# Two tokens a partition: pairing the chunks of two sequences in a recurrence-and-FFN kernel

## Chip, cores, metric

One core of one Trainium2 chip. The metric is the device time of one execution in microseconds (us), as the median of several; shares, chains and waits come from one profiled execution of each kernel.

## The reference

A gated linear recurrence (4 sequences, 8 heads, 768 tokens, head size 48), then a feed-forward layer with a squared ReLU on all 3072 tokens.

```python
f = 1.0 / (1.0 + np.exp(-f_logit))
for t in range(S):
    state = f[:, :, t, :, None] * state + np.einsum('bhd,bhe->bhde', k[:, :, t], v[:, :, t])
    y[:, :, t] = np.einsum('bhd,bhde->bhe', q[:, :, t], state)
x = y.transpose(0, 2, 1, 3).reshape(B * S, H * D)      # 3072 x 384
h = np.maximum(x @ w_in, 0.0)                          # 384 x 2048
return (h * h @ w_out).astype(np.float32)              # 2048 x 384
```

The inputs lie as (sequence, head, token, 48), so one head's one token is a run of 192 bytes.

## The kernel before

The recurrence runs in 24 chunks of 128 tokens of one sequence, one token a partition. A planner lists all steps with guessed durations and fixes the order of each engine's instructions at build time; `plan.add(name, engine, us, function, after=..., take=buffers, give=buffers)` is one step. "SP" steps are DMAs issued by SyncE. PE is TensorE, DVE VectorE, ACT ScalarE, POOL GpSimd.

```python
C = 128; NCH = 24; IOB = 7             # chunks; input buffers of each kind
LOADS = [0, "i0", 1, "i1", 2, "i2", 3, "i3", 4, "o0", "o1", 5, "o2", "o3"] + list(range(6, NCH))
XBAR = 14; XBAR2 = 18                  # from these chunks on, DMA transposes instead of TensorE's
UNITS = [(0, 2), (2, 1), (3, 1), (4, 1), (5, 1)] + [(c, 3) for c in range(6, NCH, 3)]

def load(i):                           # one DMA of 128 partitions for each of f, k, q, v
    b, c = divmod(i, NC)
    for n in ("f", "k", "q", "v"):
        def fn(n=n):
            t = io.tile([C, H, D], F32, tag="io_" + n, name="io_" + n)
            nc.sync.dma_start(t, srcs[n][b].rearrange("h s d -> s h d")[c * C:(c + 1) * C])
        plan.add(f"{n}{i}", "SP", 0.45, fn, take=["io_" + n], rank=0, data=(1.07, 1024))
# ... cut: a1 (ACT: exp, ln of f), p1 (PE: prefix sums, "pc"), a2p/a2n (ACT: exp)
def vc():                              # values to bf16
    nc.gpsimd.tensor_copy(vz[i % 4], st["v", i])
# ... v1k, v1q (DVE): k and q times the exponentials, into "az"
def t2():                              # transpose of az by DMA; p2 + v2 do it on PE
    nc.sync.dma_start_transpose(st["ts", i], az[i % 4].rearrange("p h d -> p (h d)"))
# ... p3 (PE "at"), v3 (DVE mask, "am"), p4 (PE "yp"), a3 ("ys"), p6/v6 or t6 ("xT")
def p5():                              # what the chunk adds to the state, "ds"
    for pr in range(NP):
        nc.tensor.matmul(ds[:, pr, :], a[:, H + 2*pr:H + 2*pr + 2, :].rearrange("p h d -> p (h d)"),
                         vt[:, 2*pr:2*pr + 2, :].rearrange("p h d -> p (h d)"), skip_group_check=True)
# ... mm1 ("hp", ReLU "hr", square "hT"), mm2 ("op", copy "ob", store)
```

## Time and profile before

| | before |
|---|---|
| median of 3 runs | 192.04 us (192.0 to 192.1) |
| span of the profiled run | 189.8 us, clock 1.0 |
| real TensorE work, by the chain's pitches (worked out in the prediction) | 160 us |
| DMA engines | full to 152 us |

The rows, windows and chain lines that carry this stand in the prediction. Two more lines of the page, the granted clock in 40 slices and the chain of work by engine, will be needed:

```profile
PEclk9999999999999999999999999999999999999999
...
PE 75%; ACT 11%; DMA 4%; SPq 3%; DVE 3%; issue 2%
```

Three quarters of the chain that ended last is TensorE's own work. DMA is full but holds the end up by only 4%.

### The profile page before, as it was taken

The page shows a single profiled execution, that of the slowest core. Times are in us where ns is not written, and L with a number is a line of the kernel's source. Part 1 is how long each engine was busy: PE and PEld are TensorE (multiplying, and loading weights), DVE is VectorE, ACT ScalarE, POOL GpSimd, SP SyncE. Part 2 cuts the span into 40 slices and gives each one's busy share as a digit, 9 for nine tenths or more (in the row PEclk, how much of TensorE's full clock was granted, in tenths as well). Part 3 has the DMA queues.
Part 4 walks back from the last instruction along what each step waited for, and adds up shares of the span by engine and source line. Part 5 has one row for each costly group of instructions (what it writes and reads, how often), then busy time and mean ns, then how long its engine had stood idle before and what let it go on. Part 6 is the DMA issues. An engine that isn't in the chain of part 4 may idle for free.

```text
span 189.8 us, 4807 instructions
## 1 busy us (share of the span) xinstructions
PE 177.5 (93%) x1845; PEld 120.8 (64%) x1845; DVE 127.6 (67%) x259; ACT 132.8 (70%) x281; POOL 54.8 (29%) x105
## 2 busy tenths in 40 slices
PE   6978689989899999999999999999999999999992
PEld 5867478767676666665656666666565666666551
DVE  5484688668397886999988777777667764343300
ACT  4426479786676469999998986978875787565521
POOL 5451343241224561305324311531324401100000
PEclk9999999999999999999999999999999999999999
DMA  6999899999979999999799999979999762211112
GB/s 122 188 191 206 174 187 153 196 164 191 205 137 221 232 227 201 207 197 159 140 155 194 207 137 241 218 109 215 194 216 177 176 60 64 62 45 41 41 41 83
DMA packets 118646, 30.26 MB, mean 159 GB/s; under 512 B 113408, under 2 KB 117760, under 8 KB 118624
## 3 DMA queue, kind: packets, MB, share of 16 engines
q1 hardware_dynamic: 113760, 23.27, 71.2%
q0 software_dynamic: 4864, 6.69, 16.4%
q8 instruction: 14, 0.23, 0.5%
q14 instruction: 8, 0.07, 0.1%
HBM read 25.17 MB, written 4.72 MB: 157 GB/s over the span
## 4 chain that ended last, share of the span: by engine, by line
PE 75%; ACT 11%; DMA 4%; SPq 3%; DVE 3%; issue 2%
PE op L489 31%; PE hp L444 30%; ACT hr L451 4%; DMA io_f<-in_f_logit_dram 4%; SPq L215 3%; PE at L342 3%; PE yp L365 3%; PE tr L318 2%; ACT hT L458 2%; PE pc L286 2%; PE xp L379 1%; PE ds L405 1%; ACT pz L276 1%; ACT e L275 1%; DVE hr L453 1%
## 5 line engine op out<-in xcount | busy, mean ns | idle before, releaser
L444 PE MATMUL hp<-xT,w_in 128*128 128x384 bf16 (+2 forms) x528 | 78.0, 282 | 2.5 <-DVE hr L453 1.9
L489 PE MATMUL op<-w_out,hT 128*128 128x384 bf16 x384 | 76.2, 326 | 0.3 <-ACT ob L499 0.3
L451 ACT ACTIVATE hr<-hp 128x384 bf16<-128x384 f32 (+1 forms) x100 | 50.5, 509 | 20.0 <-PE hp L444 18.0
L444 PEld LDWEIGHTS <-w_in 128*128 128x128 bf16 x528 | 42.3, 98 | 20.7 <-issue 4.0
L489 PEld LDWEIGHTS <-hT 128*128 128x128 bf16 x384 | 35.1, 98 | 21.8 <-issue 0.4
L460 DVE TENSOR_TENSOR hT<-hr 128x384 bf16<-128x384 bf16 (+1 forms) x75 | 29.7, 400 | 27.7 <-ACT hr L451 26.8
L349 DVE TENSOR_TENSOR am<-at,ut 128x512 bf16<-128x512 f32 x48 | 31.6, 685 | 3.7 <-PE at L342 3.4
L422 POOL TENSOR_TENSOR sz<-tm,en 48x192 bf16<-48x192 f32 x40 | 22.0, 549 | 29.9 <-DVE tm L413 7.2
L458 ACT ACTIVATE hT<-hr 128x384 bf16<-128x384 bf16 (+1 forms) x45 | 24.8, 554 | 1.6 <-DVE hr L453 0.3
L504 POOL DMA_DIRECT2D out_dram<-ob x18 | 10.4, 577 | 47.3 <-ACT ob L499 31.2
L280 POOL CAST vz<-io_v 128x384 bf16<-128x384 f32 x24 | 13.6, 567 | 31.2 <-DMA io_v<-in_v_dram 30.7
L306 DVE TENSOR_TENSOR az<-io_k,ep 128x384 bf16<-128x384 f32 x24 | 14.0, 584 | 8.3 <-ACT ep L296 5.1
L275 ACT ACTIVATE e<-io_f 128x384 f32<-128x384 f32 x24 | 12.5, 520 | 7.7 <-DMA io_f<-in_f_logit_dram 7.7
L499 ACT COPY ob<-op 128x384 f32<-128x384 f32 x18 | 8.6, 478 | 12.8 <-PE op L489 12.7
L296 ACT ACTIVATE ep<-pc 128x384 f32<-128x384 f32 x24 | 11.7, 486 | 5.8 <-PE pc L289 5.4
L310 DVE TENSOR_TENSOR az<-io_q,en 128x384 bf16<-128x384 f32 x24 | 14.7, 614 | 0.0
L276 ACT ACTIVATE pz<-e 128x384 bf16<-128x384 f32 x24 | 12.5, 523 | 0.8
L453 DVE TENSOR_SCALAR hr<-hp 128x384 bf16<-128x384 f32 (+1 forms) x20 | 11.6, 584 | 2.0 <-PE hp L444 1.8
L522 PE MATMUL idle<-zero 128*128 128x128 bf16 x119 | 11.9, 256 | 1.0 <-DVE zero L245 1.0
L302 ACT ACTIVATE en<-pc 128x388 f32<-128x388 f32 (+1 forms) x24 | 11.8, 491 | 0.0
L326 DVE COPY ts<-tr 128x1024 bf16<-128x1024 bf16 x14 | 9.6, 687 | 3.1 <-PE tr L318 2.7
L365 PE MATMUL yp<-vz,am 128*128 128x48 bf16 x192 | 9.5, 184 | 1.3 <-DVE am L349 0.8
(40 smaller groups left out, 149.4 us busy)
## 6 DMA issues: line engine op xcount, KB each, us to landing
io_f<-in_f_logit_dram SPq DMA_DIRECT2D x24, 192.0 KB, 4.5
io_k<-in_k_dram SPq DMA_DIRECT2D x24, 192.0 KB, 4.6
io_q<-in_q_dram SPq DMA_DIRECT2D x24, 192.0 KB, 4.5
io_v<-in_v_dram SPq DMA_DIRECT2D x24, 192.0 KB, 4.5
out_dram<-ob POOLq DMA_DIRECT2D x18, 192.0 KB, 3.5
w_in<-in_moe_w_in_dram POOLq DMA_DIRECT2D x4, 384.0 KB, 7.4
w_out<-in_moe_w_out_dram POOLq DMA_DIRECT2D x4, 384.0 KB, 6.9
out_dram<-ob SPq DMA_DIRECT2D x6, 192.0 KB, 1.9
```

The source lines that it names most:

```text
L275: nc.scalar.activation(e, st["f", i].rearrange("p h d -> p (h d)"), AFT.Exp, scale=-1.0)
L276: nc.scalar.activation(pz[i % 2][:, :, :D], e.rearrange("p (h d) -> p h d", d=D), AFT.Ln, bias=1.0)
L306: nc.vector.tensor_mul(az[i % 4][:, H:, :D], st["k", i], st["ep", i])
L310: nc.vector.tensor_mul(az[i % 4][:, :H, :D], st["q", i], st["en", i][:, :HD].rearrange("p (h d) -> p h d", d=D))
L349: nc.vector.tensor_mul(t, st["at", i][x], ut4)
L365: nc.tensor.matmul(o_, w, r, start=(n == 0), stop=(n == len(ops) - 1), skip_group_check=True)
L422: nc.gpsimd.tensor_mul(nx[r, :, D * x:D * (x + 1)], st["tm", i][r, :, D * x:D * (x + 1)], st["en", i][r, HD:HD + NP].unsqueeze(2).to_broad ...
L444: nc.tensor.matmul(hp[:, x, :], w_in[:, ks, (f + x) * C:(f + x + 1) * C], xT[:, ks, lo:lo + W], start=(ks == 0), stop=(ks == KS - 1), skip ...
L451: nc.scalar.activation(hr[:, :m, :], st["hp", c0, f][:, :m, :], AFT.Relu)
L458: nc.scalar.activation(st["hT", g][:, f:f + m, lo:lo + W], hr[:, :m, :], AFT.Square)
L460: nc.vector.tensor_mul(st["hT", g][:, f:f + m, lo:lo + W], hr[:, :m, :], hr[:, :m, :])
L489: nc.tensor.matmul(st["o", i], hT[:, fs, tt * C:(tt + 1) * C], w_out[:, fs, :], start=(fs == 0), stop=(fs == FS - 1))
```

## The change

Intent: the loads' 192-byte rows are the costliest traffic, so two successive tokens go in one partition and make rows of 384 bytes. 128 tokens then fill 64 partitions, and the chunks of two sequences are stacked into a pair: 12 pairs for 24 chunks. Prefix sums, exponentials, products and transposes go by halves `r` (first or second token of a partition). The values must lie one token a partition to be multiplied, so ACT issues four SBUF-to-SBUF copies a pair. The FFN goes by units of two chunks.

```diff
-    IOB = 7
-    XBAR = 14
-    XBAR2 = 18
-    UNITS = [(0, 2), (2, 1), (3, 1), (4, 1), (5, 1)] + [(c, 3) for c in range(6, NCH, 3)]
-    GC = 3
+    IOB = 4
+    XBAR = 5
+    XBAR2 = 6
+    UNITS = [(c, 2) for c in range(0, NCH, 2)]
+    GC = 2
-                nc.sync.dma_start(t, srcs[n][b].rearrange("h s d -> s h d")[c * C:(c + 1) * C])
+                t = io.tile([C, H, 2, D], F32, tag="io_" + x, name="io_" + x)
+                for j in range(2):
+                    nc.sync.dma_start(t[P2 * j:P2 * (j + 1)].rearrange("p h r d -> p h (r d)"),
+                                      srcs[x][2 * m + j][:, c * C:(c + 1) * C, :].rearrange("h (p r) d -> p h (r d)", r=2))
-            nc.gpsimd.tensor_copy(vz[i % 4], st["v", i])
+            nc.gpsimd.tensor_copy(st["vb", n].rearrange("p r h d -> p h r d"), st["v", n])
+        def vs():
+            t = st["vz", n] = work.tile([C, 2, H, D], BF16, tag="vz", bufs=3, name="vz")
+            for j in range(2):
+                for r in range(2):
+                    nc.scalar.dma_start(t[P2 * r:P2 * (r + 1), j].rearrange("p h d -> p (h d)"),
+                                        st["vb", n][P2 * j:P2 * (j + 1), r].rearrange("p h d -> p (h d)"))
+        plan.add(f"vs.{n}", "ACT", 0.4, vs, after=[f"vc.{n}"], take=["vz"], data=(0.66, 0))
+        plan.add(f"sub.{n}", "DVE", 0.47, sub, after=[f"p1.{n}"], take=["le"], give=[f"pz:a1.{n}"])
-            nc.sync.dma_start_transpose(st["ts", i], az[i % 4].rearrange("p h d -> p (h d)"))
+                for j in range(2):
+                    nc.sync.dma_start_transpose(st["ts", n][:, j, :, r, :], a[P2 * j:P2 * (j + 1), r].rearrange("p h d -> p (h d)"))
+            for pr in range(NP):                 # ds: 16 matmuls of 64 rows a pair
+                for r in range(2):
+                    for j in range(2):
+                        z = slice(P2 * j, P2 * (j + 1))
+                        nc.tensor.matmul(ds[j][:, pr, :], a[z, r, ...], vb[z, r, ...], start=(r == 0), stop=(r == 1))
 # cut: the same by halves in a1, p1, a2, v1, p2, v2; mask and prefix matrix re-ordered; stores in two halves
```

## The prediction

> **What bounds the kernel now.** I read, in order, the engine rows and slices of the page, the windows by stage, the same windows for the feed-forward matmuls alone, the chain of work, and the trace's packet records.
>
> ```profile
> PE 177.5 (93%) x1845; PEld 120.8 (64%) x1845; DVE 127.6 (67%) x259; ACT 132.8 (70%) x281; POOL 54.8 (29%) x105
> PE   6978689989899999999999999999999999999992
> DMA  6999899999979999999799999979999762211112
> DMA packets 118646, 30.26 MB, mean 159 GB/s; under 512 B 113408, under 2 KB 117760, under 8 KB 118624
> q1 hardware_dynamic: 113760, 23.27, 71.2%
> ```
>
> Two things are full at once. The DMA engines are full for the first 32 slices (152 us), with packets nearly all under 512 B. TensorE looks full from about slice 11. That "busy" has to be checked, because the group view gives 326 ns for a 384-column matmul while the chain passes 48 of them in 7.81 us, 163 ns each. So I count TensorE work from the chain's pitches:
>
> ```profile
> 178.60 7.81 PE op L489 x48
> 27.54 1.50 PE hp L444 x24
> 29.04 0.45 PE tr L318 x8
> 29.48 0.17 PE ds L405 x4
> 37.97 0.33 PE at L342 x8
> 16.04 0.32 PE pc L286
> 57.65 0.20 PE yp L365 x8
> 34.08 0.35 PE xp L379 x3
> 7.57 7.32 DMA io_f<-in_f_logit_dram
> ```
>
> Feed-forward: 384 op at 0.163 us is 62.5 us; hp has the same columns, 62.8. Attention, by pitches (pc 0.16 + 0.08 for its small ones, tr 0.45, at 0.33, ds 0.17, yp 0.20 + 0.17, xp 0.19 where dense), times the chunks that run each on TensorE (24, 20, 14, 24, 20, 24, 20, 18), is 34.7. Together 160 us of a 189.8 us span: 30 us are lost. Where, the windows tell (all engines; then matmuls of hp, then of op, alone):
>
> ```profile
> 17.00:50.00 33.00, 27.95 (x394) 22.89 (x394) 22.02 (x43) 24.07 (x45) 9.82 (x16) 1.00 1.07 179
> 50.00:92.00 42.00, 41.79 (x490) 28.89 (x487) 36.16 (x72) 33.09 (x76) 15.41 (x28) 1.00 1.02 201
> 92.00:151.00 59.00, 58.84 (x551) 36.36 (x550) 45.60 (x93) 48.06 (x108) 19.77 (x36) 1.00 1.04 184
> 17.00:50.00 33.00, 16.05 (x198) 2.07 (x3) 10.09 (x17) 1.00 1.07 179
> 17.00:50.00 33.00, 4.07 (x19) 0.00 (x0) 0.48 (x1) 1.00 1.07 179
> ```
>
> Priced by the pitches, TensorE does 25.7 us of real work in the first 50 us (the rest is filler on the tile "idle", or waiting), 134 us in the 136 us to 186, and then 3.7 us of last copy and store. So the loss is 24 us in the first 50, 2 later, 4 at the end. The first 50 us are bound by DMA: chunks, counted by 192-byte packets, are in at 5.9, 10.3, 20.6, 26.5, 35.9, 44.4 and 49.4 us; the eight weight pieces at 13.0, 16.0, 19.3, 28.9 (w_in) and 32.4, 35.8, 42.5, 45.9 (w_out). After 50 us TensorE is the bound, with DMA full beside it.
>
> **What the Trainium skill says.** "DMA: Bandwidth & Descriptors", Specifications, puts the minimum transfer for line rate at 512 B. The trace agrees that small ones are dear: a 192-byte packet takes 17.4 ns on average, 11 GB/s, a 1536-byte store packet 64 ns, 24 GB/s. The same page, Rules for kernel authors, says two transfers to disjoint partition halves gain nothing over one; the change splits each load so, and no run yet shows what that costs. The same page, "Issuing engines are not separate DMA queues", says DMAs of ACT run on the same 16 engines and spare only issue time: so the new SBUF copies are extra load on a full resource. "TensorEngine Tiling (Array Packing)" offers two row tiles for contract sizes up to 64; the trace agrees: the 64-row "at" matmuls go at 41 ns for 128 columns in pairs, where a 128-row transpose takes 56.
>
> **The change, part by part.**
> Loads: 98,304 packets of 192 B become 49,152 of 384 B. At 17.4 ns the old ones take 107 us of all 16 engines. For 384 B I interpolate between 192 B and 1536 B: 17.4 + 192 x (64-17.4)/1344 = 24 ns, so 74 us. A chunk falls from 4.45 to about 3.1 us: minus 33 us of DMA.
> DMA added: 3,072 packets of 768 B for re-laying the values, some 37 ns by the same line, 7 us; transposes move from 10 chunks to 14 (ts) and from 6 to 12 (xT), 12,544 to 18,944 packets at 30 ns, plus 12 us. Net minus 14 of some 167 us.
> TensorE: ds becomes 16 half-row matmuls a pair at about 42 ns, 0.67 us for 0.34, ten times: plus 3.4. Transposes leave it: 4 x 0.45 + 6 x 0.17: minus 2.8. Feed-forward in units of 256 columns is the same columns. Net plus 0.6: 160.4 us.
> DVE and ACT: a subtraction a pair, 12 x 0.55, plus 6.6 us; four fewer PSUM copies at 0.69 and six at 0.36, and fewer, fuller evictions (96 tiles of 512 columns against 120 smaller ones), minus some 12. ACT issues four DMAs a pair; a 128-packet store issue on SP took 0.33 us, so some 1.2 us a pair, 14 us in all, that no busy row counts.
>
> The path that decides is the start. By hand, with the order of instructions of the changed program: pair 0 lands at about 9 us instead of 5.9 for a chunk; its f at 4.4. The exponentials (0.84 + 2 x 0.52), the prefix matmul, four products of 0.56, two transposes through one bank with a 0.69 copy each, four mask products of 0.68 and a state copy of 0.55 x 2 are more serial work on DVE before the first pair can be multiplied: 19 us against 17.1 for the first hp. In ACT's order the re-laying of pair 1, which waits for its v, stands before a copy of pair 0's xT; with the weights sharing the engines (in the trace they took some 60% while both flowed) that v lands near 20, so the first hp comes at some 24 us. Then weights: all six remaining pieces are issued after pair 1's v, so the last w_in is in at about 29, the last w_out at 44. Loads: pair 2 at 35, pair 3 at 47: eight chunks where it was six. In TensorE's order the eight op of the second half of chunk 0 stand behind that last w_out. So at 44 us TensorE has done the first two pairs' hp (10.4), one chunk's op (2.6) and three pairs' attention (9.3): 22.3 us, as much as before by then (22). But from there four chunks wait with op and pair 2 with hp, and TensorE can be dense six us sooner than before.
> Span: 44 + (160.4 - 22.3) + some 3 of small stalls + 3.7 = 188.8; the timed run is 2.2 longer than the span: 191.0.
>
> **Rivals.**
> 1. DMA is the real bound and the saved 14 to 33 us show: then pairs land early, TensorE is dense from 35 us, and the time is 184 to 187. For: DMA full for 152 us. Against: TensorE was dense from 50 us anyway; only the start can pay, and there weights are half the traffic.
> 2. A new wait on ACT or SP. Issue time of the re-laying (14 us) and its waiting for v in ACT's fixed order hold back evictions of hp, which has two banks of 0.65 us; a DMA transpose took 1.2 us or more of SP to issue whatever its size, and there are now six a pair, 7 us of a 13.3 us pair, beside eight load issues. One us lost a pair makes 200 to 204. For: ACT was 94 to 96% busy from 70 to 100 us. Against: the xT still has another group's op work to hide behind.
> 3. Transposes from 64 partitions write shorter runs; if a packet took twice as long, DMA in the second half would need 17 us a pair against TensorE's 13.3 and the end would slip by 10 us or more. Nothing in the profile before shows it.
>
> **Range and chances.** The main sum gives 191.0. The start is uncertain by 4 us either way (when weights and loads share), the stalls by plus 4. So 187 to 196. Faster by 2% needs under 188.2: the start must go as in rival 1, 0.25. Slower by 2% needs over 195.9: rivals 2 and 3, 0.18. Within 2%: 0.57.
>
> **What would show it.** Right: 384-byte packets near 24 ns; first hp after 19 us; TensorE dense from some 44 us with 138 us of work left; weights done near 44. Wrong on the fast side: first hp by 17 us, or dense before 38. Wrong on the slow side: hp waiting for ACT evictions while ACT waits on DMA issues or on vb, TensorE gaps over 5 us in all after 50 us, or transposes that land later than the 3.9 us of before. DMA load per pair in the second half should be near 13 us.

## The result, and the profile after

| | before | after |
|---|---|---|
| median (range), 4 runs each on the same chip | 192.02 us (191.35 to 192.1) | **230.8 us** (229.82 to 231.23) |
| ratio, 95% interval | | 1.2021 (1.1973 to 1.207), slower |
| span of the profiled run, mean clock | 189.8 us, 1.0 | 228.8 us, 0.939 |

A ratio here is the mean time of one kernel's runs over that of the other's of the same rounds, so it is not quite the ratio of the medians quoted. Executions over 1.5% slower than the fastest of the same kernel are left out of the means. Results were right.

From the page of the changed kernel: TensorE, granted clock and DMA in 40 slices of 5.7 us, the packets, the main queue, the chain by engine and by line.

```profile
PE   7747377996998892995979589799749999999991
...
PEclk9995559999999999799999979999988999999999
DMA  6999899969729698796996699999999873121112
...
DMA packets 81175, 34.28 MB, mean 150 GB/s; under 512 B 72576, under 2 KB 80576, under 8 KB 81152
...
q1 hardware_dynamic: 71872, 24.92, 60.0%
...
DMA 32%; PE 28%; SPq 10%; ACT 9%; ACTq 5%; issue 5%; DVE 4%; POOL 4%; POOLq 0%; DVEq 0%
DMA io_v<-in_v_dram 16%; DMA vz<-vb 12%; PE op L575 12%; PE hp L530 11%; ACTq L310 5%; SPq L226 5%; SPq L390 4%; POOL vb L303 4%; ACT hr L537 2%; DMA ts<-az 2%; DMA io_q<-in_q_dram 2%; DVE az L355 2%; ACT e L296 1%; PE at L453 1%; ACT ep L344 1%
```

The packets of the main queue did fall, from 113760 to 71872. But DMA, which was full, has holes from slice 9 on, and TensorE has holes to slice 30. The chain has passed from TensorE (75%) to DMA (32%), and to SP and ACT while they issue; by line, loads of v (16%) and the new copies (12%, and 5% for their issue, L310) lead. Half-clock slices (5 tenths) stand where TensorE had been idle. The windows by stage, with the columns as in the prediction (engines' busy time, clock, DMA share, GB/s):

```profile
17.00:50.00 33.00, 25.12 (x297) 19.73 (x298) 20.27 (x38) 17.70 (x35) 7.81 (x10) 0.75 1.09 195
50.00:92.00 42.00, 33.76 (x379) 23.96 (x374) 27.25 (x55) 25.11 (x50) 13.03 (x19) 0.99 0.79 166
92.00:151.00 59.00, 49.63 (x540) 35.44 (x539) 36.23 (x69) 35.29 (x71) 16.11 (x23) 0.95 0.92 166
```

In the 42 us after 50, TensorE is busy 33.8 us (before: 41.8) and the DMA share is 0.79 (before: 1.02). Both resources that were full are now idle for part of the time. DMA did not get less to do: added up from the packet records, its packets took 185.6 us of all 16 engines, where they had taken 167.6 (the loads alone 98.0, where 74 were predicted and 107 had been); but its share fell all the same. For TensorE this is neither more work nor, outside the half-clock stretches, slower work, but waiting. Priced by pitches as in the prediction, with `ds` at the 0.33 us that its 16 matmuls took, the longer span falls so:

| TensorE lost (time less real work) | predicted | measured |
|---|---|---|
| to the point where it should be dense (44 us predicted; 50 us for measuring) | 21.7 | 31.4 |
| from there to the end (measured: to 190 us) | 3 | 35.1 |
| the end | 3.7 | 5.1 |
| work itself | 160.4 | 157.1 |
| sum = span | 188.8 | 228.8 (rounded) |

What do the loads wait for? The waits of SP's queue (who waited, line; for what; us in total, times, longest). L226 issues the loads:

```profile
SPq L226 <- DMA vz<-vb: 26.2, 10, 9.0
...
SPq L226 <- DMA io_v<-in_v_dram: 11.6, 13, 2.3
```

A load of new inputs needs nothing from a re-laying copy, and yet SP waits 26.2 us for such copies to land. In the kernel before, where L215 issues the loads, the longest entry of its load line is

```profile
SPq L215 <- POOL sz L422: 2.8, 3, 1.9
```

On the other engines, first of the kernel before, then of the changed one:

```profile
POOL vz L280 <- DMA io_v<-in_v_dram: 30.7, 14, 6.6
```

```profile
POOL vb L303 <- DMA io_v<-in_v_dram: 49.7, 8, 10.7
...
ACT e L296 <- DMA vz<-vb: 11.3, 3, 5.7
```

ACT, too, is seen to stand until copies land ahead of `e`, which reads nothing of them; the issues of the next copies, which wait for their turns, lie in between. The chain that ended last, in order of time (start, duration, what), shows the circle:

```profile
73.55 4.96 DMA vz<-vb
78.58 3.38 DMA io_v<-in_v_dram
...
84.31 0.84 POOL vb L303
85.17 0.48 ACTq L310
85.68 0.61 ACTq L310
86.33 0.68 ACTq L310
87.05 0.66 ACTq L310
```

A copy lands; then a load of v is issued and lands; POOL casts it; then ACT issues four copies; and so on.

The reason stands in the program's own listing, which the build of the kernel puts out. Every DMA issued by SP or ACT signals on one of eight semaphores, DMAHW0 to DMAHW7, which it takes in turn in the order of the program; a DMA waits until the previous user of its semaphore has landed. All 196 DMAs of SP and ACT in the changed kernel, stores and transposes too, follow this order in the listing. Below are successive issues of each engine in the changed kernel, with their waits:

```
SP   L226 DMACopy io_f<-in_f_logit_dram 64x8x96 [waits DMAHW0_49]
SP   L226 DMACopy io_f<-in_f_logit_dram 64x8x96 [waits DMAHW1_49]
SP   L226 DMACopy io_k<-in_k_dram       64x8x96 [waits DMAHW6_49]
SP   L226 DMACopy io_k<-in_k_dram       64x8x96 [waits DMAHW7_49]

ACT  L310 DMACopy vz<-vb 64x384 [waits DMAHW2_49,Pool_49]
ACT  L310 DMACopy vz<-vb 64x384 [waits DMAHW3_49]
ACT  L310 DMACopy vz<-vb 64x384 [waits DMAHW4_49]
ACT  L310 DMACopy vz<-vb 64x384 [waits DMAHW5_49]
```

SP's numbers jump from 1 to 6: turns 2 to 5 belong to ACT's copies. The next load that takes number 2 waits for a copy to land, and ACT issues that copy only when it reaches it in its fixed order, after POOL's cast. In the kernel before, SP has the eight to itself while it loads: eight loads in flight, two chunks. In the changed one eight half loads are one pair, the same bytes; but four turns in twelve are ACT's.

### The profile page after: what moved, and what is told of

It reads as the page before. It is cut to its first block, busy times and chain, and to the rows that moved or that the text cites. A ratio compares the mean times of both kernels' runs of the same rounds, so it can differ in the third digit from the quotient of the medians.

```text
span 228.8 us, 4956 instructions
## 1 busy us (share of the span) xinstructions
PE 187.2 (82%) x1913; PEld 136.9 (60%) x1913; DVE 126.6 (55%) x244; ACT 123.8 (54%) x237; POOL 59.3 (26%) x108
## 4 chain that ended last, share of the span: by engine, by line
DMA 32%; PE 28%; SPq 10%; ACT 9%; ACTq 5%; issue 5%; DVE 4%; POOL 4%; POOLq 0%; DVEq 0%
DMA io_v<-in_v_dram 16%; DMA vz<-vb 12%; PE op L575 12%; PE hp L530 11%; ACTq L310 5%; SPq L226 5%; SPq L390 4%; POOL vb L303 4%; ACT hr L537 2%; DMA ts<-az 2%; DMA io_q<-in_q_dram 2%; DVE az L355 2%; ACT e L296 1%; PE at L453 1%; ACT ep L344 1%
## 5 line engine op out<-in xcount | busy, mean ns | idle before, releaser
L530 PE MATMUL hp<-xT,w_in 128*128 128x256 bf16 x576 | 78.5, 276 | 3.5 <-ACT hr L537 3.3
L537 ACT ACTIVATE hr<-hp 128x512 bf16<-128x512 f32 x86 | 50.7, 594 | 33.9 <-PE hp L530 24.2
L530 PEld LDWEIGHTS <-w_in 128*128 128x128 bf16 x576 | 55.5, 99 | 19.3 <-issue 5.3
L546 DVE TENSOR_TENSOR hT<-hr 128x512 bf16<-128x512 bf16 x73 | 32.9, 456 | 40.8 <-ACT hr L537 40.4
L593 POOL DMA_DIRECT2D out_dram<-ob x36 | 19.3, 541 | 60.6 <-ACT ob L585 53.8
L460 DVE TENSOR_TENSOR am<-at,mask 128x512 bf16<-128x512 f32 x48 | 31.3, 682 | 4.1 <-PE at L453 4.0
L296 ACT ACTIVATE e<-io_f 128x768 f32<-128x768 f32 x12 | 10.1, 841 | 28.6 <-POOL sz L436 13.9
L303 POOL CAST vb<-io_v 128x768 bf16<-128x768 f32 x12 | 10.4, 867 | 54.6 <-DMA io_v<-in_v_dram 49.7
L436 POOL TENSOR_TENSOR sz<-tm,en 48x384 bf16<-48x384 f32 x20 | 17.0, 849 | 24.1 <-DVE tm L423 10.2
L544 ACT ACTIVATE hT<-hr 128x512 bf16<-128x512 bf16 x23 | 14.4, 633 | 0.6
```

The lines of the kernel that those rows point to most:

```text
L296: nc.scalar.activation(e.rearrange("p h r d -> p (h r d)"), st["f", n].rearrange("p h r d -> p (h r d)"), AFT.Exp, scale=-1.0)
L303: nc.gpsimd.tensor_copy(st["vb", n].rearrange("p r h d -> p h r d"), st["v", n])
L436: nc.gpsimd.tensor_mul(nx[r, :, :, D * x:D * (x + 1)], tm[r, :, :, D * x:D * (x + 1)], g.unsqueeze(3).to_broadcast([D, 2, NP, D]))
L460: nc.vector.tensor_mul(t, st["at", i][x], mask.rearrange("p y s t -> p y (s t)"))
L530: nc.tensor.matmul(hp[:, x, :], w_in[:, ks, (f + x) * C:(f + x + 1) * C], xT[:, ks, lo:lo + W], start=(ks == 0), stop=(ks == KS - 1), skip ...
L537: nc.scalar.activation(hr[:, :m, :], st["hp", c0, f][:, :m, :], AFT.Relu)
```

## The experiments

The theories: the re-laying hurts through the turns of the semaphores; or through ACT's time for issuing, or ACT's waiting for v; or the transfers of 64 partitions cost the loads; or the DMA transposes occupy SP. The bracket after a time is the median of the kernel before on the same chip. The first edits show what was changed; buffer releases that follow from it are cut. The median 195.14 in brackets is of four runs, two of them slow; ratios use fast runs alone.

**No re-laying (e2_no_relay).** Attention reads the values as they lie, so the result is wrong (relative error 1.0); everything else stays.

```diff
-        plan.add(f"vs.{n}", "ACT", 0.4, vs, after=[f"vc.{n}"], take=["vz"], data=(0.66, 0))
+        plan.add(f"vs.{n}", "POOL", 0.01, lambda: st.__setitem__(("vz", n), st["vb", n]), after=[f"vc.{n}"])
```

> The changed kernel without the re-lay copies at all: the values are used as they stand (wrong result on purpose, same shapes and work otherwise). Theory A and C: 190-203 us, a few us below the run with copies from POOL, by the 7-10 us of DMA time and the copy's latency. Theory B: 215 or more.

Measured: 206.73 us (205.48 to 209.79) [192.89], ratio 1.0702 (1.0635 to 1.0769). That lies between the ranges of the theories (190 to 203, and 215 or more). So the copies account for 24 of the 38.8 us, and 14 are left. SP's queue no longer waits for any DMA at its load line. The work done by 50 us is some 25 us again, nearly that of the kernel before; the first hp comes at 26.8 us, where it was 33.3 in the changed kernel.

**The copies on GpSimd's queue (e1_relay_pool).** Right result. In the listing these copies take turns on other semaphores, DMASW0 to DMASW7, and SP's loads go through DMAHW0 to 7 without a gap.

```diff
-                    nc.scalar.dma_start(t[P2 * r:P2 * (r + 1), j].rearrange("p h d -> p (h d)"),
+                    nc.gpsimd.dma_start(t[P2 * r:P2 * (r + 1), j].rearrange("p h d -> p (h d)"),
```

> The changed kernel with one thing moved: the SBUF copies that re-lay the values are issued by POOL (software queue, its own completion semaphores) instead of ACT. In the changed kernel SP's loads stood waiting for these copies (26.2 us in ten waits) because all DMAs of SP and ACT take turns on eight completion semaphores, and a load waits until the last DMA on its semaphore has landed. Theory A (loads chained to re-lay copies through shared semaphores): SP's waits for vz vanish, v loads are issued a pair or more ahead, the time falls from 231 to 195-208 us. Theory B (the 384-byte packets at 32 ns do not free DMA, so DMA bandwidth is the bound): at most 5 us off, 225 or more. Theory C (ACT stands waiting for v in its fixed order): falls as in A, as ACT no longer waits for vb; e2 and a later run must tell C from A.

Measured: 218.97 us (217.21 to 220.23) [192.89], ratio 1.1345 (1.1253 to 1.1438): half of the 24 us is gone; neither theory A (195 to 208 us) nor B (225 or more) foresaw that. The other half shows as waiting: TensorE for the copies, and SP at a transpose (L390) that stands in its order ahead of the loads. Part of this waiting is new: the copies now take turns with POOL's weights and stores, their issues waited 6.6 us for w_out pieces to land, and one copy took 17.4 us to land (median 4.1). From the waits of the engines, then of SP's queue:

```profile
PE yp L476 <- DMA vz<-vb: 15.2, 3, 10.5
```

```profile
SPq L390 <- DVE az L355: 22.8, 4, 16.2
```

**ACT waits but does not issue (e8_relay_pool_act_waits).** e1, and a one-column copy on ACT that reads the cast values where the issue stood, so that ACT waits for v as in the changed kernel.

```diff
+            nc.scalar.copy(dt, st["vb", n][:, 0, 0, :1])
+        plan.add(f"dm.{n}", "ACT", 0.4, dummy, after=[f"vc.{n}"])
```

> The run with the re-lay issued by POOL (219.0 us), plus one tiny ACT copy a pair that reads vb, so that ACT again stands waiting for v in its fixed order as in the changed kernel, without issuing DMAs and without the shared semaphores. Changed kernel 230.8. If ACT's waiting for v is what POOL's issue took away (theory C): 226-232. If it was ACT's issue time (31 us) and the semaphores shared with SP (theory A): 217-222.

Measured: 217.06 us (215.11 to 218.29) [193.29], ratio 1.1252 (1.1165 to 1.1339). The interval overlaps that of e1: ACT's waiting for v is not what costs, at least where the shared turns are gone.

**ACT busy nearly as long as the issues took (e13_relay_pool_act_busy).** e1, and four ACT copies of 128x384 a pair in that place.

```diff
+            for y in range(4):
+                nc.scalar.copy(dt, st["vb", n][:, y % 2].rearrange("p h d -> p (h d)"))
+        plan.add(f"dm.{n}", "ACT", 0.4, dummy, after=[f"vc.{n}"])
```

> The run with the re-lay on POOL (219.0 us) plus four ACT copies a pair of some 0.5-0.6 us each, at the place where the changed kernel has its four issues: ACT loses the time of the issues (31 us in all), no DMA and no semaphore of SP is touched. If the issue time is what makes the changed kernel 12 us slower than that run: 227-233 us. If it is the shared semaphores (SP's loads waiting for the re-lay): 217-223.

Measured: 221.23 us (220.77 to 223.07) [195.14], ratio 1.1453 (1.1309 to 1.1597), some 2 us above e1, and the intervals overlap. The 48 copies took 24.6 us of ACT. The issues did take long in the changed kernel. In the view of one line, min/median/max in ns, first and last start:

```profile
L310 ACTq DMA_DIRECT2D vz<-vb x48: 468/608/2032, 12.2 to 185.0; - x48
```

Together they held ACT for 31.3 us; but 24.6 us of extra work in ACT cost about 2 us in the end, if anything. Both e8 and e13 start from e1, which waits for its copies anyway; without such waits ACT's time might count for more, and no run shows that.

**The copies issued by ACT, but read by nobody (e14_unread_relay).** e2, and ACT still issues the four copies a pair into a tile that nothing reads. Its output is wrong, which doesn't matter for the time.

```diff
+        plan.add(f"vx.{n}", "ACT", 0.4, vs, after=[f"vc.{n}"], data=(0.66, 0))
+        plan.add(f"vs.{n}", "POOL", 0.01, lambda: st.__setitem__(("vz", n), st["vb", n]), after=[f"vc.{n}"])
```

> The run without re-lay (206.7 us; wrong result on purpose), but ACT issues the same four copies a pair into a tile that nobody reads. No matmul waits for them; only ACT's issue time, the DMA load and the eight shared semaphores are back. If these are what the re-lay costs: 218-228 us, with SP waiting for these copies. If the cost is that the product waits for the data: 206-211.

Measured: 231.96 us (230.01 to 232.85) [195.14], ratio 1.1956 (1.1747 to 1.2165). That is above the 218 to 228 expected: the whole 24 us are back, although no instruction uses what the copies bring. So attention's wait for the values is not needed for the loss; the copies' place among the other DMAs is enough. SP's queue again waits for them:

```profile
SPq L226 <- DMA vz<-vb: 25.0, 11, 7.3
```

**The same, from a constant (e15_unread_constant).** e14, but the copies read a constant tile. They still stand after the cast in the plan, but no longer wait for it on the chip. This was to break the circle load, cast, copy, load.

```diff
+    vk = const.tile([C, 2, H, D], BF16)
-                                        st["vb", n][P2 * j:P2 * (j + 1), r].rearrange("p h d -> p (h d)"))
+                                        vk[P2 * j:P2 * (j + 1), r].rearrange("p h d -> p (h d)"))
```

> As the run with the unread copies (232.0 us), at the same places in ACT's order, but the copies read a constant tile instead of the values just cast, so they need not wait for v. Same number of DMAs, bytes, ACT issues and turns on the eight semaphores; only the link from a pair's v to the loads that follow is cut. If the loop (load of v, cast, copy, next load on that semaphore) makes the loss: 207-216 us. If it is the number of DMAs, their issue time on ACT or fewer loads in flight: 225-233.

Measured: 229.33 us (227.6 to 230.97) [193.59], ratio 1.1855 (1.1771 to 1.1939). I had expected 207 to 216: missed. The circle through v is not needed.

```profile
SPq L226 <- DMA vz<-vk: 27.4, 10, 5.1
```

A copy that depends on no data still holds the loads up for 27.4 us. ACT's issue time and the bare number of DMAs, which the expectation names beside the turns, are in e13 too (221.2 us). What is left is that SP's turn comes after ACT's, and ACT arrives there when its own order of work lets it.

**The kernel before with such copies (e4_before_with_relay).** The same number of copies, 48 of 64 partitions, in the old layout: two a chunk, issued by ACT. Right result.

```diff
-            nc.gpsimd.tensor_copy(vz[i % 4], st["v", i])
+            nc.gpsimd.tensor_copy(st["vb", i], st["v", i])
+        def vs():
+            for r in range(2):
+                a = slice(64 * r, 64 * (r + 1))
+                nc.scalar.dma_start(vz[i % 4][a].rearrange("p h d -> p (h d)"), st["vb", i][a].rearrange("p h d -> p (h d)"))
+        plan.add(f"vs.{i}", "ACT", 0.2, vs, after=[f"vc.{i}"], take=["vz"], give=[f"vb:vc.{i}"], data=(0.33, 0))
```

> The kernel before plus a re-lay that changes nothing in the layout: the cast values go through an SBUF to SBUF copy of two 64-partition DMAs a chunk, issued by ACT, as in the changed kernel. Right result. Theory A and C: the old kernel now shows SP waiting for the copies and slows by 5 to 20% (202-230 us). Theory B: the copies add some 7-10 us of DMA time to an engine set that is full until 150 us, hidden behind TensorE: 192-197 us.

Measured: 215.94 us (214.92 to 218.55) [192.89], ratio 1.1183 (1.1106 to 1.126). The copies cost 23 us without any pairs or halves. Its profile fell in a slow run (218.55), so I take only dependencies from it. Here the same turns act in the other direction. In the chain in order of time, ACT's issue of a copy (L287) is released by the landing of a load of q, which it does not read:

```profile
72.55 5.80 DMA io_q<-in_q_dram
78.43 0.47 ACTq L287
78.93 2.17 ACTq L287
```

ACT, which evicts for TensorE, stands behind SP's loads; SP's queue in turn waits at the transposes for what ACT and DVE make (34.2 us for az). It does not wait for the copies at its load line, which I had expected. Which engine is seen to stand differs from kernel to kernel.

**The kernel before with half loads (e5_before_half_loads).** 192-byte rows stay; each load is issued as two DMAs of 64 partitions. Right result.

```diff
-                nc.sync.dma_start(t, srcs[n][b].rearrange("h s d -> s h d")[c * C:(c + 1) * C])
+                for j in range(2):
+                    nc.sync.dma_start(t[64 * j:64 * (j + 1)], srcs[n][b].rearrange("h s d -> s h d")[c * C + 64 * j:c * C + 64 * (j + 1)])
```

> The kernel before with each load issued as two 64-partition halves (192-byte rows as before): eight semaphores now hold one chunk in flight instead of two. Theory A in its stronger form (fewer bytes in flight hurts by itself): 3 to 8% slower, 198-207 us. If only the link to the re-lay matters: 192-196 us. Theory B says 192.

Measured: 215.07 us (214.08 to 216.38) [192.89], ratio 1.116 (1.1092 to 1.1228). That is more than the 198 to 207 us expected. Packets did not become slower (17.1 ns on average, before 17.4). What rose is the number of issues. Of the kernel before, then of e5, one load line (min/median/max ns):

```profile
L215 SPq DMA_DIRECT2D io_f<-in_f_logit_dram x24: 449/862/3354, 0.7 to 142.6; - x24
```

```profile
L216 SPq DMA_DIRECT2D io_f<-in_f_logit_dram x48: 595/633/2417, 0.7 to 168.9; - x48
```

The smallest issue took 0.45 us for 128 partitions and 0.60 for 64. By the medians an issue of 64 partitions was the shorter one (0.63 against 0.86); only together are the two halves dearer. In e5 SP spends 142 us on 192 load issues and 24 on transposes (before: 108 on 96, and 22.5), which fills 92% of its time to the last load (before: 85%), and from 50 to 110 us chunks land about every 6 us (before, from 50 to 90: every 4.7). POOL's waiting for v rises from 30.7 us to

```profile
POOL vz L281 <- DMA io_v<-in_v_dram: 79.5, 21, 7.9
```

So halving the loads is dear by itself. It adds to SP's issue time and also halves how many bytes eight semaphores keep in flight; this run does not separate the two.

**The kernel before with wide rows alone (e6_before_wide_rows).** One whole DMA of 128 partitions brings 256 tokens of one sequence in rows of 384 bytes; the kernel takes each half as if it were a chunk, so the result is wrong. It shows what wide rows can give at best.

```diff
-                nc.sync.dma_start(t, srcs[n][b].rearrange("h s d -> s h d")[c * C:(c + 1) * C])
+                nc.sync.dma_start(t.rearrange("p h r d -> p h (r d)"),
+                                  srcs[n][b][:, c * C:(c + 2) * C, :].rearrange("h (p r) d -> p h (r d)", r=2))
```

> The kernel before with only the rows widened: one DMA of 128 partitions brings two chunks of a tensor in rows of 384 bytes (tokens land in another order, so the result is wrong on purpose; the work is the same; the prefix matmul may run two chunks ahead instead of three, for the planner). It tells whether 384-byte packets are dear by themselves or because a 64-partition half writes to half the partitions. In the changed kernel a 384-byte packet took 32-35 ns where 24 were predicted, so the loads gained nothing. Theory P (the half loads are the cause): packets near 20-24 ns here, DMA under 80% busy in the middle, time 182-192. Theory Q (384-byte rows cost twice 192-byte rows whatever the shape): packets 32-35 ns, time 190-198.

Measured: 189.7 us (188.22 to 190.77) [193.29], ratio 0.9836 (0.9759 to 0.9914). Its TensorE and DMA rows:

```profile
PE   7784998999999999999999999999999999999992
...
DMA  5999999999999999995998604407253321111112
```

DMA has room from slice 22, where the kernel before was full to slice 32 (its packets took 133 us of all engines, before 167.6), and yet the time falls only by 1.6%: TensorE was dense anyway after the start. A 384-byte packet of a whole load took 26.3 ns on average here, 27.9 in e9 and 28.6 in e10 below; of a half load 31.9 in the changed kernel, 31.5 and 31.6 in e14 and e15, and 34.8 to 35.9 in e1, e2, e7, e8 and e13. The medians do not part so cleanly (22 to 26 for whole loads; 22, 26 or 35 for halves). The stores that SP issues do: a 1536-byte packet took 64 to 66 ns in whole stores (the kernel before, e4, e5, e6) and 98 to 100 in the half stores of all other runs.

**Pairs without copies and with whole loads (e9_no_relay_whole_loads).** e2, and each load is one DMA of 256 tokens of one sequence; wrong. One DMA for a pair of two sequences does not build: the access pattern has too many dimensions.

```diff
-                for j in range(2):
-                    nc.sync.dma_start(t[P2 * j:P2 * (j + 1)].rearrange("p h r d -> p h (r d)"), ...)
+                nc.sync.dma_start(t.rearrange("p h r d -> p h (r d)"),
+                                  srcs[x][(n % 12) // 3][:, (n % 3) * 256:(n % 3 + 1) * 256, :].rearrange("h (p r) d -> p h (r d)", r=2))
```

> The run without re-lay (206.7 us), with each load as one 128-partition DMA instead of two halves (rows of one sequence, wrong result on purpose). SP issues 48 loads instead of 96 and eight semaphores hold two pairs in flight instead of one. Theory I (SP's issue time and the semaphores of the halves are what is left): 188-197 us, loads issued well ahead in the second half. Rival (what is left is order and latency of the pairs themselves: PSUM banks, transposes): 202-208 us.

Measured: 194.09, 197.14, 197.73 and 200.6 us [193.29]. The last three are slow against the first, so there is no ratio; its profile, too, is of a slow run. Of e2's 206.7 us some 6 to 13 go with the halves, and with the bytes in flight, which double.

**Pairs of one sequence (e10_same_seq).** The correct form of that: a pair is two successive chunks of one sequence, one whole load for each input, the copies on GpSimd's queue as in e1, the state passed on within the pair.

```diff
+                nc.sync.dma_start(t.rearrange("p h r d -> p h (r d)"),
+                                  srcs[x][n // 3][:, (n % 3) * 256:(n % 3 + 1) * 256, :].rearrange("h (p r) d -> p h (r d)", r=2))
-            row = ((2 * (n // NC) + j) * NC + n % NC) * C
+            row = i * C
 # cut: state and its two steps by chunk, not by pair
```

> A repair with the right result: the pair is two chunks that follow each other in one sequence, so a tensor of a pair is one 128-partition load in rows of 384 bytes (48 loads instead of 96 halves); the re-lay is issued by POOL; the state passes from the first half to the second within a pair. Against the run with the re-lay on POOL (219.0 us) it takes away the halves only. If the halves cost DMA time (35 against 22 ns a packet) and SP time: 203-212 us. If the re-lay's latency and the transposes on SP are all that is left: 215-220.

Measured: 209.39 us (208.6 to 209.88) [195.14], ratio 1.0809 (1.0669 to 1.095). 9.6 us below e1, on another chip; the ratios, 1.1345 and 1.0809, say the same. So the halves cost that much in a right kernel too; the state's passing and the bytes in flight change with them and were not parted from them. This is the fastest right form of the pairs that I found. The kernel before beats it.

**Transposes by DMA two pairs later (e11_same_seq_xbar7).** e10 was seen to stand at a transpose for az for up to 20.0 us.

```diff
-    XBAR = 5
-    XBAR2 = 6
+    XBAR = 7
+    XBAR2 = 9
```

> The repair with DMA transposes from pair 7 (ts) and pair 9 (xT) on, as in the kernel before (chunks 14 and 18), which takes 8 + 6 issues of 1.2-1.4 us off SP and their load off the DMA engines, and gives TensorE 4 x 0.45 + 6 x 0.19 = 2.9 us. I expect 198-208 us: 3 us or more under the repair alone, still above the kernel before, since the re-lay stays. Rival: TensorE's added work shows fully and it is 1-3 us slower than the repair.

Measured: 210.98 us (210.39 to 211.5) [195.14], ratio 1.0904 (1.08 to 1.1008). No gain, and by the runs of this chip a loss of 1.6 us, as the rival had it; my expectation missed. That wait is where SP stands, not why it stands.

**No DMA transposes (e7_no_relay_pe_transposes).** e2 with all transposes on TensorE; wrong like e2.

```diff
-    XBAR = 5
-    XBAR2 = 6
+    XBAR = 99
+    XBAR2 = 99
```

> The run without re-lay (206.7 us), with all transposes on TensorE (XBAR and XBAR2 out of reach), so SP issues no transposes (28 + 12 of them, 55 us of its time in the run without re-lay) and never stands waiting for az ahead of a load. TensorE gets 14 x 0.45 + 12 x 0.19 = 8.6 us more work. If SP's queue paces the second half: 198-206 us, loads ahead by 5 pairs. If it does not: 212-218 us.

Measured: 203.69 us (203.15 to 204.6) [193.29], ratio 1.0558 (1.05 to 1.0617); e2 had 1.0702. Faster by 3 us, on another chip, with ratios that do not overlap, although TensorE has 8.6 us more work. A DMA transpose holds SP for at least some 1.2 us whatever its size: 28 `ts` took 38.4 us of SP and 12 `xT` 16.6 us in the changed kernel, where the kernel before spent 22.5 on both.

## Why the prediction was wrong

Predicted 191.0 us, measured 230.8, outside the range of 187 to 196, with the likeliest class missed.

**The step that failed** is how the added DMAs were priced. The prediction took them as load ("3,072 packets ... 7 us") and as ACT's issue time ("14 us in all"), and allowed "some 3 of small stalls" after the start. The runs put in its place a coupling of the issuing engines: the copies take turns with the loads on eight semaphores. With the copies gone, 24 of the 38.8 us go (e2); with copies that nobody reads, all are back (e14), even from a constant (e15); ACT's time alone brings about 2 and its waiting alone none (e13, e8). Moved to a queue outside the eight, half of the 24 remains, in part as new waiting behind the weights (e1). What no run did is give the copies semaphores of their own on ACT's queue; so that the turns are the cause is shown by SP's 26.2 us, by the listing and by exclusion of the rivals, not by a run that removed nothing else.

**The second mis-sized term** is the half load. The prediction priced its packets by interpolation at 24 ns. That is near for whole transfers (means of 26 to 29 ns) and wrong for the halves that the change uses (31.9 in the changed kernel, 35 without ACT's copies). So the loads gave DMA 9 us back (107 to 98) and not 33, and where the prediction has "net minus 14", all packets together took 18 us more (167.6 to 185.6). Halves also leave SP with 96 load issues, as many as before, where whole loads would have had 48. Against whole loads that is 9.6 us (e1 against e10, with the reserve made there). It had quoted the skill's rule on halves and written that no run showed the cost yet, and then used the whole-transfer figure.

Point by point:

- *Bound before.* Right. e6 frees DMA some ten slices earlier and gains 1.6%: only the start can pay, as said. The expected gain of 1.0 us was of the right kind; there was little to be had.
- *TensorE's work.* 160.4 predicted (its own terms, 160.0 and 0.6, add up to 160.6), 157.1 measured by the same pitches: `ds` took 0.33 us for its 16 matmuls, not 0.67.
- *The start.* First hp at 24 predicted, 33.3 measured. The pairs were to land at 9, 20, 35 and 47 us; they landed at 10.0, 22.7, 42.7 and 54.5. Without copies (e2) it is 10.1, 21.7, 34.1 and 48.4: nearly the predicted series. The by-hand order was good; what it lacked was the coupling. Of its signs for the slow side, gaps of TensorE after 50 us came (35.1 us lost to 190), but hp hardly waited for ACT's evictions (3.3 us in all). The last w_out piece was predicted at 44 and came at 49.7.
- *DMA per copy packet.* 37 ns predicted, 53.9 measured, 10.4 us in all: too small to matter.
- *ACT's issue.* 14 us predicted, 31.3 measured, worth about 2 (e13).
- *Rival 1* (DMA the real bound, 184 to 187 us) fell, though not by the change itself, which gave DMA no relief (185.6 us of packets, before 167.6). e6 settles it: 133 us of packets, and 1.6% faster.
- *Rival 2* came nearest: "a new wait on ACT or SP", 200 to 204 us. Its kind was right, its size (8 to 12 us more) a fifth to a third of the truth, and its cause, one us a pair of issue time and evictions held back, is the small part. Its remark on SP holds: transposes cost SP 1.2 us each, and removing them all gains 3 us net (e7).
- *Rival 3* (slow transposes from 64 partitions) fell: `ts` landed in 3.3 us at the median (before 3.9), `xT` in 4.2 (before 3.3); a 256-byte packet took 26.3 ns, before 30.4.
- *The clock.* The changed kernel ran at half clock from 16.4 to 33.5 us and in three later stretches of 3.4 us, each after TensorE had been idle. "TensorE: Matmul & The Clock Gate" of the Trainium skill, in its part on the HAM clock gate, states half rate after an idle window of about 3.4 us. The stretches of 3.413 us fit a window of that length; but the gaps in TensorE's records before the four stretches were 2.8, 4.4, 3.2 and 4.3 us, so two were shorter. Half rate follows from the waiting and adds to it. Priced by pitches, 8.4 us of work fell in these stretches, so it can have added at most about that (an estimate); in e2 it was 6.1 us.

What remains between the pairs without copies and halves (e9) and the kernel before is 0.8 us by the one fast run and 4 us by the median of all four; it was not settled.

Two places of the skill bear on the cause. "DMA: Bandwidth & Descriptors", section "Issuing engines are not separate DMA queues", adds to what the prediction took from it that initiating DMAs on multiple engines "will only save the time on the sequencer it takes to initiate the DMA, which is usually small relative to the DMA itself". Here a copy was issued in 0.61 us and landed in 4.0 (medians), which agrees; but ACT's 48 copies held up SP's loads (26.2 us of waits), which that sentence does not warn of. Its section "Why a DMA increments its semaphore by 16 and not by 1" advises one semaphore per slot in flight. The eight turns do just that; what the copies cost here, 24 us, shows that it can be dear when two engines with different orders share the slots.

## What to carry to other kernels

Before adding small DMAs on another engine, look in the program's listing at which semaphores they take turns on: a cheap copy can hold up every load behind it until its engine comes to it. Two transfers over halves of the partitions are not one transfer cut in two: price the issues of both, and measure the packets of the half form itself. When two full resources both show holes after a change, look for a wait in the queues of the issuing engines before any busy time.

## What the Trainium skill lacked or had wrong

- "DMA: Bandwidth & Descriptors", "Issuing engines are not separate DMA queues": it lacks that DMAs of SP and ACT, as built here, share eight completion semaphores in program order, so that one engine's copy delays the other's load (26.2 us of SP's waits; unread copies raised the time from 206.7 to 232.0 us). No page that I read has it.
- The same page, Rules for kernel authors: the rule against halves gives no cost; what the skill has on half the partitions ("SBUF — State Buffer", Door 1) are bandwidths, also of two halves at once, but no issue times and no times of packets this small. Here a 64-partition load took at least 0.60 us to issue against 0.45 for 128 partitions, a 384-byte packet 31.5 to 35.9 ns on average against 26.3 to 28.6, a 1536-byte store packet 98 to 100 against 64 to 66, a 192-byte packet the same (17.1 against 17.4); splitting the loads of the kernel before made it 11.6% slower.
- The same page, Specifications: below 512 B it gives no times (a later section counts cycles for 256 B, and measures nothing). Here 192 B took 17.4 ns, 384 B 26 ns (means, whole transfers): 11 and 15 GB/s for each engine.
- The same page, DMA Transpose (X-bar): that section gives no issue time (the page's part on trn3 B0 has a table of cycles). Here SP was held for at least about 1.2 us for each, with 1024, 512 or 384 packets alike.
- "TensorE: Matmul & The Clock Gate", the HAM clock gate: two of the four idle gaps before half rate were shorter (2.8 and 3.2 us, by matmul records) than the window of about 3.4 us stated. Nothing else in the places named above was contradicted by a run.
